# A gated two-filter spectral mixer on one core: a new planned order, weight rows sorted onto two DMA queues, inverse matrices loaded first

## The chip, the cores and the metric

The kernel runs on one core of one Trainium2 chip. The core has a matrix engine (TensorE, PE in the profile; its weight loads are the row PEld), a vector engine (VectorE, DVE), an activation engine (ScalarE, ACT), GpSimd (POOL) and SyncE (SP). In this kernel POOL and SP compute nothing and only issue DMA transfers, each on a queue of its own; the queues share 16 DMA engines. The metric is the device time of one execution in microseconds (us), lower is better. Several executions of a kernel are shown with their median.

## The reference

The input `x` has 2048 rows of 1024 numbers. Two filters A and B share it: a real 2-D Fourier transform, a product with a complex weight array of 2048 x 513 (one array for the real part, one for the imaginary part), and the inverse transform. A gate per row mixes the two results.

```python
def _A_ref(x, w_r, w_i):
    X = jnp.fft.rfft2(x.astype(jnp.float32), axes=(-2, -1))
    X = X * (w_r + 1j * w_i)
    return jnp.fft.irfft2(X, s=(S, D), axes=(-2, -1)).astype(jnp.bfloat16)
...
x = A_x
g = sigmoid((x * gate_w).sum(-1, keepdims=True))
a = _A_ref(x, A_w_r, A_w_i)
b = _B_ref(x, B_w_r, B_w_i)
return g * a + (1 - g) * b
```

## The kernel before, in words

The transforms are matrix products with constant cosine and sine matrices. The row axis of 2048 is split into 128 x 16, and everything is bf16 with sums in PSUM (8 banks). The stages, by the names of the code:

- **x loads and S1.** Eight DMAs bring `x` in 512 KB pieces (two of the 16 row groups each). DVE folds each piece (`fS`, `fT`, for three of them `f2`), PE transforms along 128 rows with the matrix F (`S1`, 16 calls), ACT or DVE evicts to R3 (`Z`). The gate's sums run beside it (`gate`, `zg`).
- **D and S2.** For each `sq` of four: four calls `D` (8 matmuls of 256 columns, along the 1024 axis, with the matrix DM), evicted as `Q`; then two calls `S2` (16 matmuls of 512 columns, along the axis of 16, matrix SK), evicted as `X`; and a little extra step for the Nyquist column, `qx` on DVE, `S25` on PE, eviction `X5`.
- **Products.** `prod(b, m)` multiplies the spectrum with the weights of filter `b` (0 is A, 1 is B): two DVE instructions of 128 x 2052 each, 32 in all (16 for A, 16 for B). The products of A and of B lie in a few tiles each that an I1 must free before the next can be written.
- **I1 and turns.** `stage_i1(b, m)` is 64 matmuls of 512 columns (the inverse along the axis of 16), 16 calls in all; each is evicted in two pieces `V` of 128 x 1024. Each piece is then moved across partitions by two DMAs of 128 KB from SBUF to SBUF (`turn0`, `turn1`), 64 in all. Those of the half h = 0 are issued on SP, those of h = 1 on POOL, and at most three per queue are under way (TD). The turns of A write over R3, so they wait for the last `D`.
- **Gate matrices.** `gmix` (PE call `gm`, sigmoid on ACT, `RA` and `RB` on DVE) folds the gate into the inverse matrix RM.
- **S1i, Di and output.** For each of 16 row groups and two halves c, `S1i` (8 matmuls of 128 columns), eviction `G`, `Di` (4 matmuls of 256 columns, matrix DI), eviction `o`; DVE combines the halves (`h0`, `h1`, `y0`, `y1`) and SP issues the output DMA.

**Weights.** `wpart` issues the weight loads. The arrays are cut into row groups (WSPLIT: three for A, four for B), real and imaginary part `c`, halves `J` of the partitions (0 to 63, 64 to 127), and `odd`. With `odd` = 0 rows are read rising, so that 32 long contiguous runs go to 32 partitions; with `odd` = 1 rows are read falling (negative stride), runs of one row of 1026 bytes. There are 56 loads, 128 KB each (256 KB in A's third group). The queue is chosen by `"pool" if J ^ c else "sp"`: each queue carries rising and falling rows of both halves, in the same order. POOL's loads of A wait for one x piece (`"xg"`, rows 10 and 11); all loads of B wait until `x` has been read, since they overwrite it. WLATE and WEARLY add a wait only for a fifth group, which there isn't.

**RM and DI.** The two inverse matrices, 512 KB each, are issued by SP in the loop over UNITS, at the second and the fifth I1 call of B (RMLATE); each waits for that call.

**The order.** The instructions of an engine run in the order in which `Plan.run` puts them out. It is a list scheduler that runs while the kernel is built: each of 548 nodes has costs for the engines that may run it, the ready node with the lowest priority in RANK (two base-36 digits per node) goes first, and ENGS may fix whether ACT (`a`) or DVE (`d`) evicts. The planner also models the fetch of PE's instructions: a matmul counts as two instructions (with its weight load), a call has one more, and after FETCH[0] instructions a new block begins every FETCH[1] = 256 instructions; two blocks may begin no closer together than FETCH[2] us while the former began before FETCH[3] us, and FETCH[4] us after that. The planner's model has no effect on the chip but through the order.

Of the kernel before, what the change touches and what calls it, by code (L numbers as in the profile page):

```python
# [17 lines left out]
CELL = 512  # L18
WSPLIT = (((0, 4), (4, 8), (8, 16)), ((0, 4), (4, 8), (8, 12), (12, 16)))
RANK = (  # L20
    "9p7c5d5e5f5h5i5j5k5m5o1n5q5s5t5u5x5y5z60626364666768696a6c6e6f6g6h6i6j6k6m6o6rb3bvf3en2zdbbq0o0e0c0m0t1s2u1k1c211f32ab2w"
    "1x462m53as3e4d9i4m9zb63p7vb88kbsbi571a59amc7bactbn9m9vaobddvc5ehbpeletexdleue8f50f790b3ybf9r5pdaaj9feof0e3090w22312y3r3m"
    "4e02dg0a3f0v0zac1i203u4h4q4r4u5n6y6z0jdw12cb484jd34o5wbz76cd7pce8ocr9e15e225ec6l70ef7o7wd2apd8b5dqcjeqcu2nf1cierbuc1f2c6"
    "c8828385868788898a8b8d8e8f8g8h8i8j8l8n8p8q8r8s8t8u8v8w8x8y8z9091920u16171j03000d08010h0k040n101r1e1b23282i2v2x181g1d241h"
    "1q2a1u1w2b3o2e2r3s373a3h3t2c2f3x4v3b4z542s747j6q779a7g3v4041424k7r9g7z7u9l984s9h9q9nag9w9y5a5b5l6b6nal9xana06tawa2axa89j"
    "6p6x7y8173btb0byb48mafazbe95c3bkcfbxbgc4ewf49bcoc9cvch9s9ccwckd0claedjd5e1dia1a3b7edduegeia4a5bmbobrcccsczd7dfdmdsf6f7dd"
    "2g2k2pdk3n61c0dp4yaadyeadteme00705060p0r0l14110y0x271o131m2j1t391v0i0g0s192h3g1y262q4b2o2d304c2t2l344f3c5c354n0q1p3z364x"
    "3l4938523w4t3d6u44553j714a653i561l1z5g3k72585v43785r6v457d6d7k4g7f7a6w3q7q33297m4l7n7i994p7x8caq4w8097bh50939k7e4i7sa947"
    "cm759u9ocq7laka6cx7taradcy94avah7h519dbb7bd496b1aydcaib2bcdeatc2cadrb9cncp846sbld6cge5dnd1d9ekdodhdza79tbwe6dxepe4eeesey"
    "e7evezaubjejebe9")  # L30
ENGS = (
    "-------------------------------------------------a-a---a-----a-----------a---------a-----a-a---------a--d---------a-d-d-"
    "a--d--a--a-d-a-d----d--a------d-d-a----a---a-a-d-a-a--a--a-a-----------------------------------------d------d-------a--a"
    "---a--a----------a---a------------------------------a------------a----------a------a------------d----a-d----------------"
    "----------------a-a-d-d-a-d---a------d-------a-a---a------d-d-d-d-a-a---a------d---d-d-a---a--------d-------a-a---------"
    "-a-a-a-a-a-a---a----------a-a-------a--------a-a------------a-------")
FOLD2 = (10, 12, 14)
SPLIT = ()
UNITS = ((0, 0), (0, 1), (1, 0), (2, 0), (3, 0), (1, 1), (2, 1), (3, 1))
TD = 3  # L40
PAIRS = {"warm": 12, "S2": 16, "I1": 64, "S25": 8, "gate": 8, "zg": 4, "gm": 4, "S1i": 8, "S1a": 4, "S1b": 4, "Di": 4}
WLATE = 1
BLAG = 6
WEARLY = 3
RMLATE = (1, 4)
FETCH = (120, 256, 5.5, 57.0, 4.3)
DEPTH = ((0, 2), (2, 4), (4, 6), (6, 8), (8, 10), (10, 12), (12, 14), (14, 16))


# [237 lines left out]
class Plan:  # L287
# [28 lines left out]
    def run(self, keys):  # L316
# [19 lines left out]
        dma_free = {}  # L336
# [43 lines left out]
        now, count, done = 0.0, 0, 0  # L380
        while done < len(nodes):
            for e in ("sp", "pool", "pe", "act", "dve"):
                if free[e] > now + 1e-9:
                    continue
                hold = False
                for item in ready[e]:
                    n = item[2]
                    if hold and any(t.at is None and self.limit[t.pool][0] == "ps" for t in n.tiles):
                        continue
                    if not take(n):  # L390
                        if e == "pe" and sum(self.limit[t.pool][0] == "ps" for t in n.tiles) > 1:
                            hold = True
                        continue
                    occ, lat = n.engs[e]
                    n.eng, n.start = e, now
                    free[e] = now + occ
                    n.end = now + lat
                    if e == "pe":
                        k = 2 * PAIRS.get(n.name, 8) + 1
                        t, left, c = now, occ, pc  # L400
                        pc += k
                        while FETCH[0] + FETCH[1] * len(enter) <= pc:
                            b = FETCH[0] + FETCH[1] * len(enter)
# [51 lines left out]
def bass_gated_mix__spectral_gfnet__spectral_gfnet__prompt_kernel(  # L455
# [22 lines left out]
    DI = sb("DI", 2048)  # L478
# [71 lines left out]
    def cload(eng, t, off, key, a, b, keys, more=(), **kw):  # L550
        dma("c_" + key, eng, lambda: [(ap(t, off, [[1, b - a]]).bitcast(dt.uint16), cst[key].ap()[:, a:b])],
            (b - a) * 256e-6, 400, list(more), keys, **kw)
# [260 lines left out]
    def turn(b, m, h, c, v, old, more=()):  # L813
# [2 lines left out]
        last = TURNS[h][-TD:]  # L816
        TURNS[h].append(("V", b, sq, th, h, c))
        dma("turn%d" % c, ("sp", "pool")[h], lambda: [(AP(TV[b], (64 * h + sq) * pt + th * 8192 + c * 512, [[4 * pt, 16], [1024, 8], [1, 512]]),
                                                       rg(v, 0, [[1, 512]]))], 0.131, 118, [(v, 0, 1)] + list(more) + last[:len(last) == TD], [("V", b, sq, th, h, c)], after=old)

    for sq in range(4):
        for j in range(4):
# [10 lines left out]
    for n, (sq, th) in enumerate(UNITS):  # L833
# [127 lines left out]
```

## Time and profile before

| what | value |
|---|---|
| median of 3 runs | 131.64 us |
| lowest, highest run | 129.02, 132.07 us |
| the profiled execution: time | 130.14 us |
| the profiled execution: span of the profile | 128.3 us |
| mean granted TensorE clock in it | 0.962 |
| instructions | 4406 |
| HBM read, written | 15.01 MB, 4.19 MB |

The span is the part between the first and the last instruction of the profiled execution; its own time is 1.8 us longer. The page gives the busy time of every engine, and the same in 40 slices of the span as a digit of tenths; PEclk is the clock that the matrix engine was granted. "issue" is time in which an engine waited for nothing that the profile shows. In views of groups, the text in brackets or behind the bar is the idle time ahead of the instruction and what ended it. All helpers' instructions have few lines (L501 every matmul, L504 every DVE product, L526 and L527 evictions, L536 every DMA), so they are told apart by operands: PS<-R,SK 64*32 is I1, PS<-RING,SK 64*64 is S2, PS<-DM,R with 256 columns is D, PS<-DI,RING is Di, and R<-RING DMAs are turns.

### The profile page before, as it was taken

The page shows a single profiled execution, that of the slowest core. Times are in us where ns is not written, and L with a number is a line of the kernel's source. Part 1 is how long each engine was busy: PE and PEld are TensorE (multiplying, and loading weights), DVE is VectorE, ACT ScalarE, POOL GpSimd, SP SyncE. Part 2 cuts the span into 40 slices and gives each one's busy share as a digit, 9 for nine tenths or more (in the row PEclk, how much of TensorE's full clock was granted, in tenths as well). Part 3 has the DMA queues.
Part 4 walks back from the last instruction along what each step waited for, and adds up shares of the span by engine and source line. Part 5 has one row for each costly group of instructions (what it writes and reads, how often), then busy time and mean ns, then how long its engine had stood idle before and what let it go on. Part 6 is the DMA issues. An engine that isn't in the chain of part 4 may idle for free.

```text
span 128.3 us, 4406 instructions
## 1 busy us (share of the span) xinstructions
PE 107.8 (84%) x1908; PEld 74.5 (58%) x1908; DVE 106.0 (83%) x141; ACT 95.6 (74%) x126; POOL 33.3 (26%) x66
## 2 busy tenths in 40 slices
PE   6999995999999878398976887795899999999510
PEld 2388854976678433133443453343799999999200
DVE  1489998487789999972999999966869679999990
ACT  4599998477777996468979779835553769999930
POOL 0001999990000003111534413114443000000000
PEclk9999999999999999859999999999779999999995
DMA  4999999999999999920767796468767100545654
GB/s 112 410 423 412 404 229 230 230 218 232 229 222 250 235 244 246 253 89 24 240 197 241 216 270 170 139 187 280 235 217 240 49 0 5 245 193 212 252 244 170
DMA packets 13926, 27.89 MB, mean 217 GB/s; under 512 B 2481, under 2 KB 8625, under 8 KB 13778
## 3 DMA queue, kind: packets, MB, share of 16 engines
q1 hardware_dynamic: 10752, 19.18, 47.9%
q0 software_dynamic: 3008, 8.40, 25.7%
q8 instruction: 15, 0.25, 0.9%
q14 instruction: 5, 0.04, 0.1%
q10 hardware_dynamic: 146, 0.02, 0.1%
HBM read 15.01 MB, written 4.19 MB: 150 GB/s over the span
## 4 chain that ended last, share of the span: by engine, by line
PE 38%; DVE 35%; ACT 9%; DMA 7%; issue 7%; SPq 1%; DVEq 1%
PE PS L501 38%; DVE RING L504 19%; DVE R L504 15%; ACT RING L526 5%; ACT R L526 5%; DMA R<-in_A_x_dram 4%; DMA R<-RING 3%; SPq L536 1%; DVEq L244 1%; DVE FM L527 0%
## 5 line engine op out<-in xcount | busy, mean ns | idle before, releaser
L526 ACT ACTIVATE RING<-PS 128x1024 bf16<-128x1024 f32 (+1 forms) x59 | 52.1, 939 | 14.5 <-PE PS L501 14.5
L526 ACT ACTIVATE R<-PS 128x1024 bf16<-128x1024 f32 (+2 forms) x55 | 42.5, 845 | 8.9 <-PE PS L501 8.9
L504 DVE TENSOR_TENSOR R<-R 128x2052 bf16<-128x2052 bf16 x32 | 37.0, 1226 | 3.3 <-PE PS L501 3.3
L501 PE MATMUL PS<-R,SK 64*32 64x512 bf16 x1024 | 30.7, 384 | 6.0 <-DVE R L504 4.4
L501 PE MATMUL PS<-DM,R 128*128 128x256 bf16 (+1 forms) x256 | 32.2, 250 | 1.0 <-ACT R L526 1.0
L536 POOL DMA_DIRECT2D R<-RING x32 | 16.9, 529 | 53.1 <-DVE RING L504 20.5
L501 PEld LDWEIGHTS PS<-DM,R 128*128 128x128 bf16 x256 | 26.3, 108 | 3.8 <-ACT R L526 1.5
L501 PEld LDWEIGHTS PS<-R,SK 64*32 64x32 bf16 x1024 | 15.1, 94 | 21.7 <-ACT RING L526 5.0
L527 DVE CAST RING<-PS 128x1024 bf16<-128x1024 f32 (+1 forms) x21 | 21.1, 1023 | 5.4 <-PE PS L501 5.3
L504 DVE TENSOR_TENSOR RING<-R 128x1024 bf16<-128x1024 bf16 (+1 forms) x34 | 20.9, 657 | 5.0 <-DMA R<-in_A_x_dram 4.5
L501 PE MATMUL PS<-DI,RING 128*128 128x256 bf16 x128 | 17.8, 282 | 1.4 <-ACT RING L526 1.4
L501 PE MATMUL PS<-FM,R 128*128 128x128 bf16 x128 | 16.6, 224 | 2.0 <-DMA R<-RING 2.0
L504 DVE TENSOR_TENSOR RING<-RING 128x1024 bf16<-128x1024 bf16 (+1 forms) x24 | 14.6, 644 | 0.1
L501 PEld LDWEIGHTS PS<-FM,R 128*128 128x128 bf16 x128 | 12.9, 101 | 2.4 <-DVE DM L504 2.1
L501 PEld LDWEIGHTS PS<-DI,RING 128*128 128x128 bf16 x128 | 11.8, 101 | 4.0 <-ACT RING L526 2.4
L527 DVE CAST R<-PS 128x512 bf16<-128x512 f32 (+2 forms) x13 | 10.5, 816 | 3.7 <-PE PS L501 3.6
L501 PE MATMUL PS<-RING,SK 64*64 64x512 bf16 (+2 forms) x160 | 10.7, 361 | 2.7 <-issue 1.7
L501 PE MATMUL PS<-R,RING 128*128 128x256 bf16 (+1 forms) x128 | 12.3, 253 | 0.5 <-DVE RING L504 0.5
L501 PEld LDWEIGHTS PS<-R,RING 128*128 128x128 bf16 x128 | 10.4, 98 | 3.2 <-DVE RING L504 1.6
L501 PEld LDWEIGHTS PS<-RING,SK 64*64 64x64 bf16 (+1 forms) x160 | 4.1, 110 | 7.3 <-issue 3.9
L536 POOL DMA_DIRECT2D R<-in_A_w_r_dram x6 | 3.6, 592 | 11.9 <-DMA R<-in_A_x_dram 11.9
L501 PE MATMUL PS<-RING 128*128 128x512 bf16 x12 | 5.1, 617 | 1.2 <-DVE RING L613 1.2
(30 smaller groups left out, 38.3 us busy)
## 6 DMA issues: line engine op xcount, KB each, us to landing
R<-in_A_x_dram SPq DMA_DIRECT2D x8, 512.0 KB, 7.3
R<-RING SPq DMA_DIRECT2D x32, 128.0 KB, 3.8
R<-RING POOLq DMA_DIRECT2D x32, 128.0 KB, 3.6
out_dram<-RING SPq DMA_DIRECT2D x7, 512.0 KB, 2.6
R<-in_B_w_i_dram SPq DMA_DIRECT2D x8, 128.2 KB, 21.2
R<-in_B_w_r_dram POOLq DMA_DIRECT2D x8, 128.2 KB, 17.3
R<-in_B_w_r_dram SPq DMA_DIRECT2D x7, 128.2 KB, 20.6
R<-in_B_w_i_dram POOLq DMA_DIRECT2D x7, 128.2 KB, 17.6
```

The costliest lines, as they stand in the source:

```text
L244: e.wait_ge(dsem[d], 16 * len(d.fns))
L501: return lambda e: e.matmul(o, l, r, start=start, stop=stop, skip_group_check=True)
L504: return lambda e: e.tensor_tensor(out=o, in0=a, in1=b, op=op)
L526: return [lambda e: e.activation(o, i, ACT.Copy)]
L527: return [lambda e: e.tensor_copy(o, i)]
L536: lambda e: [lambda q, d=d, s=s: q.dma_start(d, s) for d, s in pairs()],
```

## The change

The order is planned anew: RANK and ENGS are other strings, and FETCH has other intervals. The planner's times for DMA landings are changed too (no effect but through the order). RM and DI are issued right after the other constants, before any weights, and wait for nothing. Weight loads of rising rows all go to SP, of falling rows all to POOL, with the halves J alternating on each queue, one queue beginning with J = 0, the other with J = 1. On each queue a load waits for the landing of the load six before it (WD); the first six on POOL wait for DI. The expression in `turn` is written in another way and gives the same.

```diff
-FETCH = (120, 256, 5.5, 57.0, 4.3)
+FETCH = (120, 256, 7.2, 53.0, 3.4)
+WD = 6
-WLATE = 1
-WEARLY = 3
-RMLATE = (1, 4)
...
-                        dma_free[e] = max(dma_free.get(e, 0.0), now + (2.3 if e == "pool" else 1.3)) + lat
-                        n.end = dma_free[e] + 0.9
+                        lead, tail = ((1.3, 1.8), 0.9) if n.name not in ("turn0", "turn1", "out") else ((1.0, 1.1), 0.5)
+                        dma_free[e] = max(dma_free.get(e, 0.0), now + lead[e == "pool"]) + lat
+                        n.end = dma_free[e] + tail
...
     cload("sp", DM, 0, "DM", 0, 2048, ["DM"])
     cload("sp", SK, 0, "SK", 0, 1152, ["SK"])
+    cload("sp", RM, 0, "RM", 0, 2048, ["RM"])
+    cload("sp", DI, 0, "DI", 0, 2048, ["DI"])
+
+    LOADS = [], []
...
-        dma("W%d%d" % (b, ci), "pool" if J ^ c else "sp", lambda: prs, (k1 - k0) * 0.0328, 106, [("I1", 0, WLATE)] if b and ci > WEARLY else ["xg"] if J ^ c and not b else [], [("W", b, ci, J, odd, c)],
+        last = LOADS[odd][-WD:]
+        LOADS[odd].append(("W", b, ci, J, odd, c))
+        dma("W%d%d" % (b, ci), ("sp", "pool")[odd], lambda: prs, (k1 - k0) * 0.0328, 106, last[:1] if len(last) == WD else ["DI"] if odd else [], [("W", b, ci, J, odd, c)],
             after=[("x", m) for m in range(16)] if b else [], n=len(prs))
...
-            for odd in range(2):
-                for c in range(2):
-                    for J in range(2):
-                        wpart(b, ci, J, odd, c)
+            for c in range(2):
+                for J in range(2):
+                    for odd in range(2):
+                        wpart(b, ci, J ^ odd, odd, c)
...
-        for i, (t, k) in enumerate(((RM, "RM"), (DI, "DI"))):
-            if n == RMLATE[i]:
-                P.key = ("in", 1)
-                cload("sp", t, 0, k, 0, 2048, [k], more=[("I1", 1, 2 * sq + th)])
```

The strings RANK (1096 characters) and ENGS (548) are new in whole. RANK's digits follow the order in which the nodes are added; so read, the Nyquist step of `sq` 0 has priority 15 (484 before) and its eviction 14 (10 before), and the I1 calls of A, of which two had the first places among PE's calls before, stand behind all calls of S2 and 11 of the 16 of D or more. Of the 152 evictions, ENGS fixes 75 on ACT and 18 on DVE (62 and 26 before) and leaves 59 to the planner (64 before); of the 64 in the last stage (`G`, `o`) it fixes 34 on ACT (27 before) and 7 on DVE (12 before).

More of the change, by code (lines that the diff above doesn't have):

```diff
@@ L20 @@
 RANK = (
[L21 to L28, printed above, removed]
@@ L29 @@
-    "cm759u9ocq7laka6cx7taradcy94avah7h519dbb7bd496b1aydcaib2bcdeatc2cadrb9cncp846sbld6cge5dnd1d9ekdodhdza79tbwe6dxepe4eeesey"
-    "e7evezaubjejebe9")
-ENGS = (
[L32 to L36, printed above, removed]
+    "034f6n6o6p6q6s6t6u6v6w016x6y70717275767778797a7b7c7d7e7f7h7i7j7l7n7p7q7r7t7u7w7x7yc4di5c5xd457741l080k0v0x1230361z1f2k32"
@@ new lines @@
+    "5f523g3l3m5y825a425z4x7m8j8g5o9m5pan8z8t0n3r7vb78ec8918u3t5w8lchajdoc5ahe4egbyeketeq5k0a1nba9o2wdwa2aiecbhc12d041k1p2o24"
+    "4g29592i0f0e191e5i1dakd22a5h2j652l9y33ap2y254i1hd8db2pdddm3jbk43c047cc4qcd5m3vb83adudx3ne2ea55dc5se06je76ze9ar3ybc3oebee"
+    "3uehej8v8w8x8y90929394959697999a9b9c9d9e9f9g9h9i9k9l9n9p9q9r9s9t9u9w9z1314181c4d050c0h070j0w4e0l0q0z0y0s1v1o1w1x2f541y11"
+    "2e2g172n6m451a2r4p372u2v343z41aa5u3w2x6r4838b48i4j3da14m3i44494o5rb5a65b3kal5n4ubdaq6b4wau6h505v608788bnbb7obm81btbz8qc9"
@@ new lines @@
+    "8s898c8d8fbucbagcfay8o9ja7abcrcnb0cqb9asb2bpdzcucscoctcvdlcwczdad5eldjeodker646feue1f1e3f2737s7z86a4a8azbibxcgcmcyf0f36k"
+    "393c0bbl8k5j2bf6bq8baef7e5a5c6060i150r0g0m23161g0t271b1m0u2c1i0d0002090o1t1j2h1q2m212z2q3s4h313b404t353x1r1s200p104a5e3e"
+    "464s633q4k51685l4n56696d4v261u3h532t626c7g58666g835g858h8a6e8pava06i28224b5d4ra3b1ad8ma9clam8naccpbe8raod3br9x3f2s4c7k5t"
+    "awd9bsb3axdebwb6bfdpc7bgbodqcebj3p5q4lbv6ac2dtckcjc3e8d0cxcaeidnd1ciendrd64y8061d784dsepdydgdvevemdh4z9v67df98edeweseyf4"
@@ new lines @@
+    "exf5ez6latafe6ef")
+ENGS = (
+    "---------------------------------------------------a-----a-----a-a-----a-----------a-------a-a---------a--d--d--a---a---"
+    "d------da-ad-------a--a-a-----a-d-a-d----da--d---a-a-d--a-a---a---------------------------------------------------------"
+    "-a---a--a-------a--a---a--a-------a---------a-------a---------------a------a-a------a----a----a------a-d----------------"
+    "--------------------a-a-a-d---a------a-a-a-a---a-d-d------a---d-d-a---a-a----------a-a-a-----a------------a-a---a-d-----"
+    "-a-a-a-a---d---a----------a---a-a-a-a------a-----a------a-----a-----")
@@ L548, in rp, with cload @@
         return ap(PR[b], t.at * NS + off, dims, p0, np_)
-    def cload(eng, t, off, key, a, b, keys, more=(), **kw):
+    def cload(eng, t, off, key, a, b, keys, **kw):
         dma("c_" + key, eng, lambda: [(ap(t, off, [[1, b - a]]).bitcast(dt.uint16), cst[key].ap()[:, a:b])],
-            (b - a) * 256e-6, 400, list(more), keys, **kw)
+            (b - a) * 256e-6, 400, [], keys, **kw)
     P.add("zero8", {"dve": (0.1, 0.2)}, lambda e: [lambda e: e.memset(ap(G8, 0, [[1, 8]]), 0.0)], [], ["G8"])
@@ L818, in turn @@
         dma("turn%d" % c, ("sp", "pool")[h], lambda: [(AP(TV[b], (64 * h + sq) * pt + th * 8192 + c * 512, [[4 * pt, 16], [1024, 8], [1, 512]]),
-                                                       rg(v, 0, [[1, 512]]))], 0.131, 118, [(v, 0, 1)] + list(more) + last[:len(last) == TD], [("V", b, sq, th, h, c)], after=old)
+                                                       rg(v, 0, [[1, 512]]))], 0.131, 118, [(v, 0, 1)] + list(more) + last[:1] * (len(last) == TD), [("V", b, sq, th, h, c)], after=old)
     for sq in range(4):
```

## The prediction

> **What bounds the kernel now.** I read the page's shares first, then the chain that ended last in order of time, then the busy time of every engine by stage, then the waits and the DMA answers.
>
> ```profile
> PE 107.8 (84%) x1908; PEld 74.5 (58%) x1908; DVE 106.0 (83%) x141; ACT 95.6 (74%) x126; POOL 33.3 (26%) x66
> PEclk9999999999999999859999999999779999999995
> ```
>
> Three engines are near each other, so no share names a bound; the clock row shows two dips. The chain of waits names the places (start, length, what):
>
> ```profile
> 52.07 1.71 issue
> 53.78 6.33 PE PS L501 x124
> ...
> 86.25 4.04 DMA R<-RING
> 90.28 0.14 issue
> 90.42 19.09 PE PS L501 x236
> ```
>
> The reader is to see two interruptions, at 52.07 (PE waits for nothing that the profile shows) and at 86.25 (PE waits for a turn), each just ahead of a dip of the clock. By stage:
>
> ```profile
> core 0: us, PE busy (x) PEld busy (x) DVE busy (x) ACT busy (x) POOL busy (x), PEclk, DMA share, GB/s
> 20.00:40.00 20.00, 18.81 (x215) 14.86 (x216) 15.28 (x17) 14.16 (x15) 8.57 (x16) 1.00 1.05 228
> 53.78:60.48 6.70, 6.27 (x143) 2.41 (x143) 3.43 (x4) 4.03 (x5) 0.53 (x1) 0.75 0.26 73
> 60.48:83.19 22.71, 18.34 (x640) 9.59 (x640) 22.68 (x21) 19.33 (x21) 8.21 (x16) 1.00 0.71 208
> 90.42:109.50 19.08, 19.08 (x240) 17.55 (x241) 15.88 (x28) 12.75 (x24) 4.19 (x8) 0.91 0.38 118
> 109.50:128.30 18.80, 11.73 (x148) 9.93 (x145) 15.70 (x30) 13.52 (x28) 0.00 (x0) 0.93 0.56 224
> ```
>
> From 20 to 40 us (D and S2) PE is the bound, 18.81 of 20.00. From 60.48 to 83.19 (I1) it is DVE with the products, 22.68 of 22.71, while PE has 4.37 to spare and ACT 3.38. From 90.42 (S1i, Di) PE is the bound, at a clock of 0.91; the last 18.80 us are a chain through DVE.
>
> **The stall at 52 us is a late block of instructions.** A line of the page on DMA queues, two stretches from the busy times by stage (matmuls done in brackets), and the timeline of PE:
>
> ```profile
> q8 instruction: 15, 0.25, 0.9%
> ...
> 0.00:45.50 45.50, 41.73 (x444) 29.82 (x444) 35.35 (x49) 36.44 (x40) 16.46 (x34) 1.00 1.01 273
> 0.00:53.00 53.00, 47.28 (x599) 32.32 (x599) 42.85 (x56) 42.52 (x46) 18.06 (x37) 1.00 1.02 270
> ...
> 45.56 3.99 PE L501 MATMUL PS<-R,SK 64*32 64x512 bf16 x128 [0.86 <-ACT R L526]
> 51.66 0.41 PE L501 MATMUL PS<-RING,SK 64*64 64x512 bf16 x3 [0.68 <-ACT R L526]
> 53.78 1.91 PE L501 MATMUL PS<-RING,SK 64*64 64x512 bf16 x13 [1.71 <-issue]
> 55.61 4.43 PE L501 MATMUL PS<-R,SK 64*32 64x512 bf16 x128
> ```
>
> Queue 8 brought 15 packets for 1908 matmuls and as many weight loads: 3816 / 15 = 254 instructions each, the 256 that the planner's FETCH assumes, or 128 matmuls. PE stopped after matmul 599, in the midst of one S2 call, where no data can be missing. The block before began 128 matmuls earlier, at number 471: 444 had run by 45.50, and 27 more at 3.99 / 128 = 0.031 us put it at 46.4. So the block took 53.78 - 46.4 = 7.4 us. Before's planner counted on 5.5, that is 46.4 + 5.5 = 51.9, just where PE came to a stop; after's counts on 7.2 until 53 us. Later, 640 matmuls in 22.71 us are 4.54 us a block with hardly an issue wait, so refills there need no more than that; 3.4 in the new plan is not contradicted.
>
> The rule against this: the Trainium skill, Runtime: NRT & Kernel Launch, section Instruction fetch mechanics, says that refills come in blocks of 256 instructions and that crossing a block costs mostly nothing that is seen. The trace agrees with the block and not with the cost here (1.71 us). By that rule a new interval is worth nothing, and the first term below is 0; this is the second rival.
>
> **The change part by part.** No matmul, product or eviction is added or removed; the terms are the waits that the order and the loads set.
>
> (1) The new interval. What it can win is the idle time at this place.
>
> ```profile
> 58.39 3.77 ACT L526 ACTIVATE RING<-PS 128x1024 bf16<-128x1024 f32 x4 [0.73 <-PE PS L501]
> 60.13 23.01 DVE L504 TENSOR_TENSOR R<-R 128x2052 bf16<-128x2052 bf16 x20 [3.27 <-PE PS L501]
> ```
>
> DVE stood 3.27 us for PE, because the half clock after the stall held up the I1 that frees product tiles. PE loses 1.71 by the stall and 6.27 x 0.25 = 1.57 by the clock of 0.75, in all 3.28. ACT is next: 6.70 - 4.03 = 2.67 spare in that stretch. Bounds: 0 (another wait takes the place) and -3.3. I take -2.7, what ACT leaves.
>
> (2) The new order. Decoded against the list of nodes, RANK moves sq 0's Nyquist step S25 from priority 484 to 15 (its eviction X5 from 10 to 14); A's I1 calls go from the first places to behind S2 and most of D. The Nyquist step is what the first product waited for:
>
> ```profile
> 39.88 0.29 PE L501 MATMUL PS<-RING,SK 128*64 128x2 bf16 x8
> ...
> 40.47 0.17 DVE L527 CAST R<-PS 128x8 bf16<-128x8 f32 x1
> 40.54 0.15 DVE L504 TENSOR_TENSOR RING<-RING,MS 128x8 bf16<-128x8 bf16 x1
> 40.68 1.23 DVE L504 TENSOR_TENSOR R<-R 128x2052 bf16<-128x2052 bf16 x1
> ```
>
> So products may begin before 40.68. A product is 23.01 / 20 = 1.15 us; DVE has 20.00 - 15.28 = 4.72 idle between 20 and 40, room for four, which would leave the stage that DVE bounds. There ACT is next after 3.38. Bounds 0 (each early product pushes an eviction that PE waits for) and -3.4; I take -1.5, a little under the middle, because PE at 18.81 of 20.00 waits for these evictions at once. That ENGS fixes 34 instead of 27 of the last stage's evictions on ACT I set at 0: ACT has 6.33 and DVE 3.2 spare of 19.08 there, and PE bounds it.
>
> (3) RM and DI leave the turn phase.
>
> ```profile
> 73.34 0.33 SPq L536 DMA_DIRECT2D RM<-c_RM  x1
> 85.19 0.37 SPq L536 DMA_DIRECT2D DI<-c_DI  x1
> ...
> SPq L536 <- PE PS L501: 1.6, 2, 1.0
> ...
> DMA to landing us min/median/max: 2.1/3.6/6.4
> ```
>
> Each waits on SP for an I1, with turns queued behind it: 1.6 us in two waits, and DI's 512 KB run beside the turn that ends the wait at 90.42. That turn took 4.04 where the fastest transfer from RING took 2.1 and the median 3.6. Bounds 0 and -1.9. I take the median, -0.5. The gap of 1.98 then is still 1.5, so I leave the half clock behind it as it is; without it 19.08 x 0.09 = 1.7 more would go.
>
> (4) RM and DI ahead of the weights, which come later.
>
> ```profile
> DMA packets 810, 2.92 MB, mean 418 GB/s; under 512 B 96, under 2 KB 96, under 8 KB 810
> ...
> 18.81 0.64 POOL L536 DMA_DIRECT2D R<-in_A_w_i_dram  x1
> ...
> R<-in_A_w_i_dram POOLq DMA_DIRECT2D x2, 256.5 KB, 13.9
> ...
> 30.00:46.00 16.00, 15.01 (x198) 10.48 (x204) 14.84 (x17) 13.28 (x14) 0.00 (x0) 1.00 1.05 234
> 54.00:61.00 7.00, 6.57 (x165) 2.58 (x165) 3.73 (x4) 4.55 (x5) 0.90 (x2) 0.77 0.25 71
> ```
>
> 1.05 MB at the 418 GB/s of 6 to 13 us are 2.5 us. A's last load, issued at 18.81, landed about 13.9 later, at 32.7; now about 35.2, ahead of 40.68 and, being the last of A, needed only after eight products, so ahead of an earlier start too. The last of B land near 54 (the rate is 71 GB/s after it), later 56 to 57; B is wanted after sixteen products, that is four after the twelve (32 - 20) done before 60.13, near 65. Cost 0; with the cover gone, +2.5.
>
> (5) Rising rows on SP, falling on POOL. The halves J still alternate on both, bytes and load count stay, POOL issues as many as before. POOL now waits for DI instead of for x rows 10 and 11, but until then the engines carry 418 GB/s of other loads, so nothing is lost but the order. Falling rows on SP go out in packets of one row of 1026 bytes, which the changed kernel has no more of; no view prices that apart. Bounds by rates: at 250 instead of 234 GB/s the 8.4 MB of weights (4 x 2048 x 513 x 2 bytes) come 2.3 us sooner, at 209 (half of 418, if both queues fall on one half of the partitions at a time) 4.3 later. I take 0.
>
> (6) The wait for the load six before.
>
> ```profile
> 40.56 1.60 SPq L536 DMA_DIRECT2D R<-in_B_w_i_dram  x1
> ...
> R<-in_B_w_i_dram SPq DMA_DIRECT2D x8, 128.2 KB, 21.2
> ```
>
> Behind the waiting load on SP and POOL stand only further loads until the turns, and these were issued behind the last load, at 48.6, already. Six loads of 0.131 MB at half of 234 GB/s are 6.7 us of transfer in flight against the 2.1 of the fastest landing, so the engines don't run dry: 0. A landing of 21.2 shortens to about 7, which delays nobody.
>
> Sum against the profiled execution of 130.14 us (span 128.3): 130.14 - 2.7 - 1.5 - 0.5 = 125.4. The median of the three runs is 131.64, 1.5 above that execution; against it 125.4 is -4.7%.
>
> **The rivals.**
>
> First, slower: the loads end late and the refills stay slow with them. The 7.4 us block fell in the load phase and the 4.54 ones after it. If the two queues lose step (POOL starts only when DI has landed) and write the same half of the partitions, 8.4 MB at 209 GB/s end near 18.5 + 40.2 = 58.7. From 53 to 58.7 the plan sends I1 calls at its 3.4 us a block and gets one per 7.4, where 4.54 is DVE's pace: 5.7 x (1 - 4.54 / 7.4) = 2.2 us. Before's stall then stays, and PE idles long enough for one more dip of 1.6: 130.14 + 2.2 + 1.6 = 133.9. It decides if the loads end after 56 or 57. For it: 1.05 MB ahead of them. Against it: each queue alternates the halves by itself, so a lost step mends within a load, and 234 GB/s is above the 209 of one half.
>
> Second, the rule above: the refill isn't what counts, and (1) gives nothing. 130.14 - 1.5 - 0.5 = 128.1. For it: 14 of the 15 refills cause no long stall. Against it: the stall inside one S2 call.
>
> Third, the change doesn't carry to the end: the early products take the place of evictions, a new PE wait stands where the old was, the half clock too, and only (3) is left, some 129.6. For it: three engines at 74 to 84%, the last 38 us, which no term shortens.
>
> **How the numbers follow.** Forecast 0.50, with its own range 120.8 (terms at their far ends without the last dip: 130.14 - 3.3 - 3.4 - 1.9 = 121.5, and part of the dip) to 128.5. The slower rival 0.18, the second 0.12, the third 0.20. The range for all is 120.8 to 134.0. About 2% is what can be told from no change here, 129.0 to 134.3 around 131.64. Faster by over 2%: the forecast 0.50 and 0.10 of the second, 0.60. Within 2%: the third, 0.02 of the second and a small part of the slower rival, 0.24. Slower: the rest of the slower rival, where its delay is greater, 0.16.
>
> **What would show it.** (1): no issue wait over 1 us on PE between 45 and 60, a clock row without the dip at 54. (2): the first 128x2052 product before 40 us, and DVE under 95% of the I1 stage. (3): no SP wait on PE, the wait ahead of the first S1i under 1.6 us. (4) to (6): the rate drops from 230 between 54 and 57 us. Wrong would make it: loads past 58, a PE wait on ACT of several us between 25 and 45, or three dips of the clock.

## The result, and the profile after

The changed kernel took 135.50 us (median of 4 runs, 134.89 to 135.89) beside 130.41 us of the kernel before (4 runs, 129.02 to 132.07): a ratio of 1.049, interval 1.043 to 1.055. It is slower by 5%, where 125.4 us had been forecast, and lies above 134.0, the upper end for all rivals. Ratios here and below, and times said to be of the kept runs, leave out the runs that a slower state of the chip lengthened; medians hold all runs. The profiled execution took 134.89 us, with a span of 133.1 us.

The engines' shares and the clock row, from the page of the changed kernel:

```profile
PE 109.7 (82%) x1908; PEld 74.8 (56%) x1908; DVE 104.1 (78%) x137; ACT 98.5 (74%) x130; POOL 34.8 (26%) x68
PEclk9999999999999968999999999999869999999995
```

The shares tell nothing, as before; the two dips of the clock are still there, the first one earlier. The timeline of PE does tell (start, length, what; in brackets the idle time ahead and its end). The changed kernel:

```profile
38.76 0.29 PE L500 MATMUL PS<-RING,SK 128*64 128x2 bf16 x8 [0.93 <-DVE RING L503]
...
40.35 3.23 PE L500 MATMUL PS<-R,SK 64*32 64x512 bf16 x109
46.84 0.83 PE L500 MATMUL PS<-R,SK 64*32 64x512 bf16 x19 [3.27 <-issue]
47.60 6.22 PE L500 MATMUL PS<-DM,R 128*128 128x256 bf16 x40
...
59.90 3.43 PE L500 MATMUL PS<-R,SK 64*32 64x512 bf16 x114 [0.81 <-ACT R L525]
...
69.72 2.36 PE L500 MATMUL PS<-R,SK 64*32 64x512 bf16 x78 [1.79 <-issue]
...
95.92 0.26 PE L500 MATMUL PS<-FM,R 128*128 128x128 bf16 x1 [2.47 <-DMA R<-RING]
```

The last call of D before the change, in the same view:

```profile
43.64 1.07 PE L501 MATMUL PS<-DM,R 128*128 128x256 bf16 x8
```

The new order sends the first two I1 calls of A (128 matmuls) ahead of the last five calls of D. After 109 of the 128, with all data there, PE stood for 3.27 us; the 40 matmuls of D behind them ran at a granted clock of 0.73 (6.22 us, where the same kernel in a later group and other new-order kernels below take 4.56), and the last D ended at 53.82 instead of 44.71. A second stop, of 1.79 us, follows at 69.72. The other 14 I1 calls begin at 59.90 instead of 55.61, the first S1i at 95.92 instead of 90.42. From there to the end it is 37.2 us, and was 37.9: the whole loss of 5 us lies ahead of S1i.

DVE's products say the same. The changed kernel:

```profile
33.98 4.65 DVE L503 TENSOR_TENSOR R<-R 128x2052 bf16<-128x2052 bf16 x4 [0.72 <-DMA R<-in_A_w_i_dram]
...
47.72 2.37 DVE L503 TENSOR_TENSOR R<-R 128x2052 bf16<-128x2052 bf16 x2 [2.48 <-PE PS L500]
...
53.86 1.31 DVE L526 CAST RING<-PS 128x1024 bf16<-128x1024 f32 x1 [2.56 <-PE PS L500]
...
59.35 4.65 DVE L503 TENSOR_TENSOR R<-R 128x2052 bf16<-128x2052 bf16 x4 [0.21 <-DVE R L526]
64.24 13.89 DVE L503 TENSOR_TENSOR R<-R 128x2052 bf16<-128x2052 bf16 x12 [0.25 <-PE PS L500]
78.94 9.21 DVE L503 TENSOR_TENSOR R<-R 128x2052 bf16<-128x2052 bf16 x8 [0.81 <-PE PS L500]
```

The first product does come at 33.98 instead of 40.68. But DVE then stands 2.48 and 2.56 us for PE, and only 8 of the 32 products are done at 59.35, where before 12 were done at 60.13. The last ends at 88.15; before it was 60.13 + 23.01 = 83.14. Those 5.0 us are the loss. The busy times of the stretch in which each kernel did its first 8 products, 27 DVE instructions from 28 us on, before the change and after it:

```profile
28.00:52.30 24.30, 22.12 (x363) 14.04 (x361) 22.07 (x27) 20.16 (x21) 2.17 (x5) 1.00 1.06 236
```

```profile
28.00:59.35 31.35, 25.47 (x388) 16.11 (x380) 23.47 (x27) 22.68 (x23) 14.64 (x27) 0.95 0.88 200
```

DVE (the third busy time behind the length) is idle for 24.30 - 22.07 = 2.2 us before and 31.35 - 23.47 = 7.9 us after.

The queues changed too. SyncE's timeline in the changed kernel:

```profile
40.31 1.92 SPq L535 DMA_DIRECT2D R<-in_B_w_i_dram  x2
53.86 1.91 SPq L535 DMA_DIRECT2D R<-RING  x3
55.81 1.38 SPq L535 DMA_DIRECT2D R<-in_B_w_r_dram  x2
57.23 1.24 SPq L535 DMA_DIRECT2D R<-in_B_w_i_dram  x2
```

Its order has the first three turns (R<-RING) ahead of the last four weight loads. The turns wait for the last D, so SP stood 11.6 us, and weights landed until 66.9 us (54.5 before). POOL has six loads behind three turns in the same way.

**Why PE stood.** Queue 8 carries the blocks of instructions, one packet each; a boundary is the matmul with which a new block begins. In every trace here the packet that follows one boundary lands before PE goes on at the next. DMA answers for the stretch from matmul 345 (38.85 us) on, one block boundary before the stop at 473, first to 43.9, then from there to 46.8:

```profile
DMA packets 362, 1.11 MB, mean 222 GB/s; under 512 B 92, under 2 KB 92, under 8 KB 362
## 3 DMA queue, kind: packets, MB, share of 16 engines
q0 software_dynamic: 229, 0.74, 68.3%
q1 hardware_dynamic: 133, 0.37, 36.4%
```

```profile
DMA packets 271, 0.67 MB, mean 231 GB/s; under 512 B 97, under 2 KB 97, under 8 KB 270
## 3 DMA queue, kind: packets, MB, share of 16 engines
q1 hardware_dynamic: 140, 0.38, 60.6%
q0 software_dynamic: 130, 0.27, 41.5%
q8 instruction: 1, 0.02, 2.9%
```

For 5 us behind the boundary no block came: both weight queues held the DMA engines at 222 GB/s. The packet ran from 43.97 to 45.31 (its record in the trace), and PE went on at 46.84: 8.0 us from boundary to boundary. Before, the stop at 52 us has the same form: boundary at 46.24, packet 51.06 to 52.37, PE on at 53.78, 7.5 us. PE's stops of over 1 us for issue fall in all traces here behind the same numbers of matmuls: 473, 599 or 600, 726 or 728, 854, and once each 1109 and 1364, that is nearly 89 + 128 k. By the planner's own count (FETCH[0] = 120, two per matmul, one per call) the boundary of 473 stands at matmul 423, some 50 earlier: it thought the boundary passed before the pair's middle (matmul 428) and saw no wait there. Its boundaries can be moved to the chip's: with 222 for FETCH[0], which puts this one at 473, and the same RANK, the planner itself arrives at 130.3 us for the new plan instead of 120.8, with a wait in the pair, and at 123.8 instead of 122.5 for the old one. These are times of the plan, not of the chip.

### The profile page after: what moved, and what is told of

Same layout as the page of the kernel before. It is cut to its first block, busy times and chain, and to the rows that moved or that the text cites. A ratio compares the mean times of both kernels' runs of the same rounds, so it can differ in the third digit from the quotient of the medians.

```text
span 133.1 us, 4412 instructions
## 1 busy us (share of the span) xinstructions
PE 109.7 (82%) x1908; PEld 74.8 (56%) x1908; DVE 104.1 (78%) x137; ACT 98.5 (74%) x130; POOL 34.8 (26%) x68
## 4 chain that ended last, share of the span: by engine, by line
PE 31%; DMA 22%; DVE 20%; issue 12%; ACT 5%; SPq 4%; POOL 2%; DVEq 0%; ACTq 0%
PE PS L500 31%; DMA DI<-c_DI 11%; DVE RING L503 11%; DMA R<-in_A_w_i_dram 7%; DVE R L503 6%; SPq L535 4%; ACT RING L525 4%; DMA out_dram<-RING 2%; DVE R L526 2%; POOL R L535 2%; DMA R<-RING 2%; ACT R L525 1%; DVE RING L526 1%; DVEq L242 0%; ACTq L242 0%
## 5 line engine op out<-in xcount | busy, mean ns | idle before, releaser
L525 ACT ACTIVATE RING<-PS 128x1024 bf16<-128x1024 f32 (+1 forms) x66 | 56.3, 925 | 21.6 <-PE PS L500 18.5
L525 ACT ACTIVATE R<-PS 128x1024 bf16<-128x1024 f32 (+2 forms) x52 | 39.7, 853 | 3.2 <-PE PS L500 3.0
L503 DVE TENSOR_TENSOR R<-R 128x2052 bf16<-128x2052 bf16 x32 | 37.2, 1224 | 4.5 <-PE PS L500 3.5
L500 PE MATMUL PS<-R,SK 64*32 64x512 bf16 x1024 | 32.0, 378 | 8.2 <-issue 6.0
L500 PE MATMUL PS<-DM,R 128*128 128x256 bf16 (+1 forms) x256 | 33.8, 260 | 1.0 <-ACT R L525 1.0
L500 PEld LDWEIGHTS PS<-DM,R 128*128 128x128 bf16 x256 | 27.4, 111 | 3.5 <-ACT R L525 1.5
L500 PEld LDWEIGHTS PS<-R,SK 64*32 64x32 bf16 x1024 | 14.6, 92 | 24.9 <-issue 9.6
L526 DVE CAST RING<-PS 128x1024 bf16<-128x1024 f32 (+1 forms) x14 | 15.4, 1109 | 7.9 <-PE PS L500 7.8
L500 PE MATMUL PS<-FM,R 128*128 128x128 bf16 x128 | 17.3, 228 | 2.5 <-DMA R<-RING 2.5
L526 DVE CAST R<-PS 128x1024 bf16<-128x1024 f32 (+2 forms) x16 | 13.7, 861 | 4.3 <-PE PS L500 4.1
L500 PE MATMUL PS<-RING,SK 64*64 64x512 bf16 (+2 forms) x160 | 9.4, 341 | 2.4 <-DVE RING L503 0.9
```

What stands on the lines that cost most here:

```text
L500: return lambda e: e.matmul(o, l, r, start=start, stop=stop, skip_group_check=True)
L503: return lambda e: e.tensor_tensor(out=o, in0=a, in1=b, op=op)
L525: return [lambda e: e.activation(o, i, ACT.Copy)]
L526: return [lambda e: e.tensor_copy(o, i)]
```

## The experiments

Four theories are named in the expectations. O: the new order costs the time. L: the loads do, being late or differently queued. Within O, later on, B: it is the late block of instructions in the early I1 pair; D: it is the order as such, since DVE's evictions come late whether or not a block is late. The kernel before ran beside each group, with medians of 132.53 (12 runs), 131.86 (19), 132.40 (25) and 131.86 (11).

The kernels that mix an order with other loads move the nodes after the planner is done; the order of PE, DVE, ACT and the turns stays as it is. `weights` puts the loads on their queues, and `relay` puts all loads of A behind the constants (`inv` are RM and DI), all loads of B behind the last fold of `x`:

```diff
     P.run(lambda n: int(RANK[2 * n.at:2 * n.at + 2], 36))
+    def weights(new, limit, gate):
...
+                    q = odd if new else J ^ c
+                    n.eng = ("sp", "pool")[q]
+                    last = hist[q][-limit:] if limit else []
+                    n.reads = last[:1] if limit and len(last) == limit else [gate] if q and not b else []
...
+    def relay(new, limit, gate, early):
...
+        o[i:i] = [n for n in ws if n.writes[0][1] == 1]
...
+        o[i:i] = (inv if early else []) + [n for n in ws if n.writes[0][1] == 0]
```

**Old order, new loads** (RM and DI first, sorted rows, limit six, all weights ahead of the turns).

```diff
+    relay(True, 6, 'DI', True)      # in the kernel before
```

> The order of PE, DVE, ACT and of the turns is that of before, instruction by instruction; only the loads are the new ones (RM and DI ahead of the weights, rising rows on SP, falling on POOL, a wait for the load six before; all weight loads stand ahead of the turns on their queues). Theory O (the new order is what costs: an I1 pair at 40 us ahead of the last five D, where a late block of instructions holds up everything): within 1 us of before, 130 to 131.5. Theory L (the loads cost, by coming later and keeping the refills slow for longer): most of the 5 us, 133.5 to 135.5.

130.45 us (4 runs), ratio 0.985, interval 0.978 to 0.992. So queued, the loads don't cost the time in the old order.

**New order, old loads.**

```diff
+    relay(False, 0, 'xg', False)    # in the changed kernel
```

> The other half: the order of PE, DVE, ACT and of the turns is the new one, the loads are those of before (no waits among them, both kinds of rows on both queues, RM and DI amid the turns behind their I1). Theory O: 133.5 to 135.5, with an issue wait of 2 to 4 us in the I1 pair near 40 us. Theory L: 130 to 131.5, and no issue wait over 1 us before 50 us.

135.73 us (4 runs), ratio 1.016, interval 1.009 to 1.023. The order alone loses, 1.6% and not the whole 5, and PE stands at the same matmul, in the timeline of PE:

```profile
46.07 1.43 PE L500 MATMUL PS<-R,SK 64*32 64x512 bf16 x19 [3.05 <-issue]
```

**New order, last weights ahead of the turns**, with the limit and without it.

```diff
+    relay(True, 6, 'DI', True)      # in the changed kernel: loads first
+    relay(True, 0, 'DI', True)      # in the changed kernel: no limit
```

> The changed kernel with its limit of six, but with the last ten weight loads moved ahead of the first six turns on their queues; nothing else. Theory O: 134.5 to 136. Theory L, if the loads queued behind the turns are what keeps the refills slow until 66 us: the issue wait near 68 us goes, 132.5 to 134.

> The changed kernel without the wait for the load six before, so that all weight loads are issued at once and stand ahead of the turns; order, queues of the rows and the early RM and DI are the new ones. Theory O: 134.5 to 136, as the changed kernel. Theory L with the limit as its cause (the last loads are queued behind turns that wait for the last D, and end at 66 us instead of 53): the loads end near 56 us and the time falls by 2 to 4 us, to 131.5 to 133.5.

Loads first: 134.62 us (4 runs), ratio 1.017, interval 1.011 to 1.023, with a wait of 2.73 us for issue at matmul 473. With the last loads ahead of the turns the stop and a loss stay; what their queueing costs isn't settled by this, since the changed kernel stands at 1.049 and 1.035 in other groups. Without the limit: 133.19 us (9 runs, without a ratio), which is in Theory L's range. There PE waits 2.34 us for the Nyquist step, the pair starts at 42.57 and takes 5.55 us at a granted clock of 0.64, the two boundaries lie 7.1 us apart, and PE doesn't stop in the pair.

**The pair moved behind the last D.**

```diff
+    pair = [n for n in o if n.key in (("IA", 0), ("IA", 1)) and n.name in ("I1", "V")]
+    pair.sort(key=lambda n: n.at)
+    pair += [n for n in o if n.name == "mul" and n.key == ("PA", 3)]
+    rest = [n for n in o if n not in pair]
+    i = max(k for k, n in enumerate(rest) if n.name == "Q") + 1
+    P.order = rest[:i] + pair + rest[i:]
```

> The changed kernel with one group moved: the first two I1 calls of A, their four evictions and the two products that reuse their tile stand behind the last D and its eviction, instead of ahead of the last five D. Nothing else is moved, loads as changed. Theory O: the last D ends near 46 instead of 53.8 us, the later I1 calls begin 3 us sooner than in the changed kernel, 131 to 133. Theory L: the place of the pair doesn't matter, 134.5 to 136.

135.09 us (4 runs, without a ratio), which is in Theory L's range, while the events are those of Theory O. In PE's timeline:

```profile
39.68 4.56 PE L500 MATMUL PS<-DM,R 128*128 128x256 bf16 x40
45.88 3.67 PE L500 MATMUL PS<-R,SK 64*32 64x512 bf16 x128 [1.64 <-DVE RING L526]
...
56.75 3.44 PE L500 MATMUL PS<-R,SK 64*32 64x512 bf16 x116 [0.81 <-ACT R L525]
62.35 2.35 PE L500 MATMUL PS<-R,SK 64*32 64x512 bf16 x76 [2.16 <-issue]
```

The last D ended at 44.2 and I1 went on at 56.75, earlier than 59.90, but a block was late two boundaries further on (behind matmul 728). Here the move of work only moved the place where a block is late.

**Without 28 of B's 32 loads**, in the new order and in the old one.

```diff
+    gone = [("W", 1, ci, J, odd, c) for ci in range(4) for J in range(2) for odd in range(2) for c in range(2) if (ci, c) != (3, 1)]
+    P.order = [n for n in P.order if not (n.dma and n.name[0] == "W" and n.writes[0] in gone)]
...
```

> The changed kernel with its whole order, but 28 of the 32 weight loads of filter B are left out (B's products then read what x left in that place, so the output isn't the reference's). If blocks of instructions come late because of the loads under way: no issue wait over 1 us in the I1 pair at 40 us, no dip of the clock near 48, the last D ends near 48.5, and 129.5 to 131.5. If a block takes 7 us whatever the loads do: the issue wait of 3 us stays, 134 to 136.

> The same 28 loads of B left out of the kernel before, with before's order (the output isn't the reference's). If blocks come late because of the loads: the issue wait at 52 us and the dip behind it go, 127 to 129.5 against 130 to 132.5 for before; this is also what the first term of the prediction (2.7 us) is worth in the old order. If not: no change within 0.7 us. Against the run above it says what the new order costs without late blocks: Theory O with late blocks as its whole cause, less than 1 us between the two; with the detour of the D calls as a cause of its own, 1.5 to 3 us.

132.37 us (4 runs), ratio 1.011 (0.988 to 1.033), and 128.87 us (10 runs), ratio 0.996 (0.979 to 1.012). The first is some 2 us less than the changed kernel took in another group (134.32); the second is 3 us under the kernel before by medians, but by its ratio no difference can be told, so what before's stop costs isn't settled. In the new one, the DMA answer for 38.6 to 40.7, just behind the boundary at matmul 345 (38.62):

```profile
DMA packets 48, 0.14 MB, mean 66 GB/s; under 512 B 17, under 2 KB 17, under 8 KB 47
## 3 DMA queue, kind: packets, MB, share of 16 engines
q0 software_dynamic: 47, 0.12, 30.2%
q8 instruction: 1, 0.02, 4.2%
```

The block began 0.6 us behind its boundary instead of 5.1 (0.2 to 0.4 at most later ones), and no wait for issue is left on PE, in the old order neither. That the loads delay the refills is so shown. But the two orders still lie 3.5 us apart (2.9 by the kept runs, 131.26 and 128.33), which theory B doesn't explain and theory D would. In the new one the pair ran at a granted clock of 0.75, without any stop:

```profile
40.59 4.83 PE L500 MATMUL PS<-R,SK 64*32 64x512 bf16 x128
```

**RM and DI early alone**, in the old order with old loads.

```diff
+    relay(False, 0, 'xg', True)     # in the kernel before
```

> The kernel before, its order and its weight loads as they were, but RM and DI loaded right behind the other constants. If that is what the new loads win in the old order (130.5 against 132.5): 0.98 to 0.99 of before, the wait ahead of the first S1i under 1.6 us. If the gain came from the sorted rows or the limit: 0.995 to 1.01.

130.78 us (10 runs), ratio 0.995, interval 0.985 to 1.004: no difference that can be told.

**The boundaries moved.** This tells B from D with order, loads and data untouched: the warm-up ahead of S1 gets 56 matmuls more in fewer columns (5696 instead of 6144), so each boundary falls 56 matmuls earlier in the work, and the one at 473 falls at 417.

```diff
-    pe("warm", [512] * 22, lambda: [mm(psl(wps, 0, [[1, 512]]), rg(warm, 0, [[1, 128]]), rg(warm, 0, [[1, 512]]), True, True) for _ in range(12)],
+    pe("warm", [512] * 22, lambda: [mm(psl(wps, 0, [[1, 512]]), rg(warm, 0, [[1, 128]]), rg(warm, 0, [[1, 512]]), True, True) for _ in range(3)] + [mm(psl(wps, 0, [[1, 64]], 0, 32), rg(warm, 0, [[1, 32]]), rg(warm, 0, [[1, 64]]), True, True) for _ in range(65)],
```

> The changed kernel with the block boundaries moved: the warm-up at the start is cut into 3 matmuls of 512 columns and 65 of 64 columns on 32 rows (12 of 512 before), so every later matmul stands 56 places further on and every boundary of an instruction block falls 56 matmuls earlier in the work. Order, loads and arithmetic are the changed kernel's. Theory B (late blocks: a refill that takes 7 to 8 us while weights load is what stops PE in the first I1 pair): the boundary now falls at about matmul 53 of that pair's 128, some 9.5 us behind the one before it, so no issue wait above 1 us in the pair, the last D ends at about 50 instead of 53.8, the rest of I1 begins at 56 to 57 instead of 59.9, and the time is 131.5 to 133 beside a changed kernel of 134.6 to 135.5. Theory D (the order itself: evictions that DVE makes late; the late block only fills time that would be lost anyway): the issue wait goes, the rest of I1 still begins at 59 or later, time 134.5 or more.

> The changed kernel itself, on the chip and in the call of the others. Both theories: 2 to 5% over the kernel before and 3 to 5 us over the old order with the new loads; this gives the size of the order's cost on one chip.

> The changed kernel with the boundaries moved by 56 matmuls, again. If the order is a gain once its late block is gone: ratio to the kernel before 0.985 to 0.995. If the order by itself is worth nothing: 0.995 to 1.01.

Shifted 130.98 us (10 runs), the changed kernel beside it 134.32 us (6 runs, ratio 1.035, interval 1.023 to 1.047): 3.3 us less by the place of the boundaries (4.7 by the kept runs, 129.30 against 134.00). The mean clock doesn't set them apart: two of the changed kernel's runs had clocks of 0.962 and 0.991 and took 133.98 and 134.02 us. Again in another group, 130.96 us (6 runs, without a ratio). To the kernel before, the first shifted measurement stands at 0.999 (0.980 to 1.018), so no gain over it is shown. PE's timeline of the changed kernel of this group, then of the second shifted run:

```profile
45.55 0.83 PE L500 MATMUL PS<-R,SK 64*32 64x512 bf16 x19 [2.47 <-issue]
46.31 4.56 PE L500 MATMUL PS<-DM,R 128*128 128x256 bf16 x40
...
56.94 3.43 PE L500 MATMUL PS<-R,SK 64*32 64x512 bf16 x114 [0.81 <-ACT R L525]
```

```profile
40.33 3.67 PE L500 MATMUL PS<-R,SK 64*32 64x512 bf16 x128
43.94 4.56 PE L500 MATMUL PS<-DM,R 128*128 128x256 bf16 x40
...
54.65 3.67 PE L500 MATMUL PS<-R,SK 64*32 64x512 bf16 x128 [0.81 <-ACT R L525]
58.89 1.91 PE L500 MATMUL PS<-R,SK 64*32 64x512 bf16 x58 [0.57 <-DVE R L503]
63.00 2.14 PE L500 MATMUL PS<-R,SK 64*32 64x512 bf16 x70 [2.20 <-issue]
```

The pair runs through, the last D ends at 48.5 instead of 50.9, the rest of I1 begins at 54.65: B holds, and D as the main cause falls. A late block is left at 63.0 (in the first shifted run at 66.47, 3.61 us).

**The same shift in the old order with new loads**, beside that kernel without it.

```diff
+    relay(True, 6, 'DI', True)      # in the kernel before, with the new warm-up and with the old
```

> The order of before with the new loads and with the boundaries 56 matmuls earlier (the same cut of the warm-up). Theory B: the boundary that stopped PE at matmul 599 (51.7 to 53.8 us before) now falls at about 543, inside the first I1 pair, some 6.5 us behind the one before it instead of 5.4: the stall shrinks to under 1 us or goes, and the time is 0 to 1.5 us under the same kernel without the shift in this call (129 to 130.5). If the refills are as late as 7.5 us, the stall only moves into the pair and the time stays within 0.5 us. Theory D makes no difference here: the same time.

> The order of before with the new loads (RM and DI first, sorted rows, a wait for the load six before, all weights ahead of the turns), measured again with more rounds. If the loads win what the first measurement showed: 1 to 2% under the kernel before, ratio 0.98 to 0.99. If that was chance of the runs: 0.995 to 1.005.

132.09 us (4 runs) with it, ratio 1.014 (0.979 to 1.049), and 131.69 us (12 runs) without. No gain of the shift by itself is seen, so the other warm-up isn't what helped the new order; the stop only moved, into the old order's pair (1.02 us for issue at 52.06). And the old order with new loads stands at 0.9995 (0.991 to 1.008) this time, so the 1.5% of its first measurement is not settled.

**Boundaries moved and the last loads ahead of the turns**, with the limit and without.

```diff
+    relay(True, 6, 'DI', True)      # in the shifted changed kernel
+    relay(True, 0, 'DI', True)      # in the shifted changed kernel: no limit
```

> The changed kernel with the boundaries moved by 56 matmuls and the last weight loads of B put ahead of the first turns on SP and POOL. If the late refill in I1 (3.61 us at 62.5 us with the boundaries moved) comes from weights that land until about 66: the loads end about 5 us earlier, that wait falls under 1.5 us, and the time is 0.5 to 2 us under the shifted kernel of this call. If refills in I1 are late for another reason (the turns' own transfers): the wait stays somewhere between 58 and 68 and the time is within 0.7 us of the shifted kernel.

> As the one before, and no load waits for the load six before it. Loads and their end as there; the queues hold more at a time, so if a refill stands behind what is queued, refills between 37 and 56 us start later (over 6 us after their boundary) and an issue wait above 1 us comes back in or behind the first I1 pair: 1 to 2 us over the one before. If the depth of the queues doesn't matter: the same time within 0.7 us.

127.83 us (4 runs), ratio 0.975, interval 0.967 to 0.983: faster than the kernel before and the changed one. That it is faster than the shifted kernel of its group isn't settled: 127.83 against 130.96 by medians, 127.69 against a single 128.04 by the kept runs. Without the limit 129.48 us (4 runs), 0.989, interval 0.980 to 0.997. PE's timeline of the first:

```profile
40.30 3.67 PE L500 MATMUL PS<-R,SK 64*32 64x512 bf16 x128
43.90 4.56 PE L500 MATMUL PS<-DM,R 128*128 128x256 bf16 x40
...
54.62 1.91 PE L500 MATMUL PS<-R,SK 64*32 64x512 bf16 x58 [0.81 <-ACT R L525]
56.85 2.14 PE L500 MATMUL PS<-R,SK 64*32 64x512 bf16 x70 [0.32 <-issue]
```

and DVE's:

```profile
33.86 4.65 DVE L503 TENSOR_TENSOR R<-R 128x2052 bf16<-128x2052 bf16 x4 [0.36 <-DMA R<-in_A_w_i_dram]
...
59.05 23.01 DVE L503 TENSOR_TENSOR R<-R 128x2052 bf16<-128x2052 bf16 x20 [0.34 <-PE PS L500]
```

PE waits for issue once, 0.32 us in the whole span, the clock row has no dip but at its end, and the last product ends at 82.06, before 83.14 of the kernel before. With the last weights ahead of the turns the late block at 63 us isn't there. Why is not shown: the loads end at 61.8 us here, and at 62.8 and 68.6 in the two shifted runs. Without the limit no block is late in the pair either, against what was expected of deeper queues. That kernel's loss has another place: A's weights land later, PE waits 1.89 us ahead of 39.97 for the Nyquist step on DVE, which stands behind A's first products, and its pair runs at a granted clock of 0.68 (5.34 us instead of 3.67):

```profile
41.56 5.34 PE L500 MATMUL PS<-R,SK 64*32 64x512 bf16 x128
```

## Why the prediction was wrong, point by point

The step that failed is term (1), "The new interval. What it can win is the idle time at this place", taken as -2.7 between bounds of 0 and -3.3. The stall of 1.71 us was not won; it came back as one of 3.27, at 43.6 instead of 52.1 us, and moving it out of its place is worth 3.3 us (134.32 against 130.98 in one group). Nor is it shown that the stall cost 2.7 us where it was: in the old order without B's loads it is gone, at a ratio of 0.996 (0.979 to 1.012). The issue wait and the dip that the prediction had named as signs against this step are both there. The diagnosis behind it was right: a block needs about 7.5 us while weights load (7.4 was worked out; 7.1 to 8.2 from boundary to boundary at the stops of over 1 us before 56 us, in eight traces). What failed is the inference that an order planned with 7.2 us would keep that distance. The planner spaces the boundaries that it believes in, some 50 matmuls off those of the chip, and the new order put an I1 pair, a dense run of instructions (128 matmuls in 3.67 us), across a real boundary in the midst of the load phase. "51.9, just where PE came to a stop" was a coincidence: by the planner's count the old plan's boundaries stand at matmuls 420 and 546, not at 471 and 599. This could have been seen blind: the prediction counted the stop at matmul 599 from the trace, but didn't lay the same count over the new order. Nor does 3.4 us a block after 53 us hold: 4.54 was read where before's loads had ended, and with weights landing until 66.9 us the block from 63.56 took 6.2 us and PE stopped for 1.79.

Term (2), -1.5: four products came earlier, from 33.98 on, as forecast. But the prediction read the ranks as the order of execution: "A's I1 calls go from the first places to behind S2 and most of D". In what the plan puts out, the first two come earlier, behind 364 matmuls instead of 444, ahead of five calls of D and four of S2. That is the pair across the boundary. The gain wasn't lost to pushed evictions, as the bound of 0 had it, but to PE: DVE idled 5.7 us more ahead of its ninth product. What the term is worth without late blocks isn't shown: with boundaries moved and loads first the last product is 1.1 us earlier than before (82.06 against 83.14), but before's stop is gone there too, and without B's loads the new order is the slower one.

Terms (3) and (4): the wait ahead of the first S1i did not go from 1.98 to 1.5, it is 2.47 (1.84 to 3.06 in the other new-order kernels whose rows were read), and moving RM and DI alone shows no difference (ratio 0.995, 0.985 to 1.004). That A's weights would be wanted later than they land fell: DVE waited 0.72 us for them at 33.98. The landing at 32.7 was worked out from a median of two POOL loads; in the trace of before A's last load, on SP, landed at 42.4 us, and at 46.7 after the change. B's last landed at 66.9, where 56 to 57 had been worked out.

Term (5), 0: from 20 to 40 us the DMA engines moved 208 GB/s against 228 before; no cost was seen by itself, since all new loads together stand at 0.985 and 0.9995 in the old order.

Term (6): "Behind the waiting load on SP and POOL stand only further loads until the turns" was wrong. With the limit, the planner put turns ahead of the last loads of both queues, and those turns waited for the last D. While the block in the pair was late, its price isn't settled (ratio 1.017 with the loads first, 1.035 without, but medians 2.1 and 1.9 us above the kernel before); once it was not, it is between 0 and 3 us and not settled either: 130.96 against 127.83 by medians of one group, 128.04 against 127.69 by the kept runs, and in the two profiled executions the first S1i comes at 89.31 and 89.24.

The rivals: the first, slower one named the right mechanism, blocks that stay slow because loads end late, for a part of the loss: it needed loads past 57 us, they ended at 66.9, and PE stopped for 1.79 us at 69.72. What it lacked is the greater stop that ends at 46.84. The second took over a rule of the Trainium skill, Runtime: NRT & Kernel Launch, section Instruction fetch mechanics, that a block's crossing costs mostly nothing. The traces agree with it when B's loads are gone, and not when they run. So it doesn't hold here. The third foresaw that a PE wait and the half clock come back, but not that they cost more than before.

Open: what holds the two orders 3.5 us apart when B's loads are left out. In the two profiled executions the first S1i comes at 90.72 and 89.38 us, and 1.2 us lie in the lower clock of the new order's pair (4.83 us instead of 3.67), whose cause isn't shown; another 1.5 us lie behind the first S1i (38.7 against 37.2 us), without a shown cause.

## What to carry to other kernels

When a plan models a resource, check its events against the trace first: count where the chip's stops fall (here 89 + 128 k matmuls) before trusting an order that is spaced by the model. Instruction refills share the DMA engines with loads (here a block began 5.1 us behind its boundary with B's loads and 0.6 without), so a dense run of small matmuls belongs where loads are done, or a few spare matmuls can move the boundary out of it. A queue limit that makes loads wait also lets other work be queued ahead of them; look at what the last load stands behind.

## What the runs showed of the hardware that was not expected

A block's transfer began mostly 0.2 to 0.6 us behind its boundary with B's loads left out, and mostly 3 to 6 us behind it with two weight queues running; it took 0.9 to 1.9 us itself, and where PE stopped for it, PE went on 1.2 to 1.6 us after it had landed. Blocks could be late again after the loads had ended, with turns under way: in the old order with new loads, whose loads end at 62.3, a packet came 3.9 us behind its boundary at 79.0, and PE stopped for 1.23. Fifty-six more matmuls in the warm-up, which compute nothing that is used, made this kernel 3.3 us faster. The time of one and the same kernel before ranged from 127.8 to 135.3 us over these groups, more than most of the effects looked for; that is why medians here are set against medians of the same group, but where another group is named.
